# One sequence of attention steps over all pairs of three chunks, beside the first layer's matmuls

## The chip, the cores and the metric

The kernel runs on one core of one Trainium2 chip. The metric is the device time of one execution in microseconds (us). The engines are PE (TensorE, matmuls; PEld is its weight load), DVE (VectorE), ACT (ScalarE), POOL (GpSimd) and SP (SyncE, which here issues every DMA). Each engine has its own sequence of instructions, set at the build.

## What is computed

Attention over tokens that share a hash bucket, and behind it two feed-forward layers. Inputs come as float32, the weights of the layers as float64:

```python
q_bits = (einsum('bhsd,dk->bhsk', q, proj) > 0)     # 2 batches, 8 heads, 768 tokens, 64 wide, 6 bits
mask = q_bucket[:, :, :, None] == k_bucket[:, :, None, :]
scores = where(mask, scale * q @ k.T, -1e9)
attn = exp(scores - max) / (sum + 1e-9)
x = (attn @ v) as 1536 tokens x 512
h = maximum(x @ w_in1, 0);            x = (h * h) @ w_out1      # 512 -> 2048 -> 512
h = x @ w_in2; g = max(h,0) + alpha * min(h,0);   out = g @ w_out2
```

## The kernel before

The 1536 tokens are four chunks of 384 (half a batch each), numbered 0 to 3. The attention of a chunk goes pair of heads by pair of heads, four pairs. A pair (class Pair, line 203) has these steps:

- prepare (line 357): load the pair after this one, hash the keys (only in chunks 0 and 2, where a batch begins) and the queries with small matmuls, split them into a high and a low part, and put them with the mask's codes into the tiles k and q, by DMAs on SP. Two steps in chunks 1 and 3, five in chunk 2.
- scores (line 378), six times, for 2 heads x 3 blocks of 128 queries: four matmuls into a score tile s, DVE's negated maximum `low` (line 389), ACT's exponential into sm with the row sum (line 392).
- p_t (line 399), twice for each block: three PE transposes of sm into an m tile, and a copy to pt by ACT or DVE (lines 411, 413).
- recip (line 431): DVE's reciprocals of the sums, a PE transpose (line 437), a DMA out and one back that spreads them over the partitions (lines 441, 444).
- av (line 415), in three parts of four matmuls, pt times V, into one m tile o; the last part copies it to u.
- finish (line 447): u times the reciprocals on DVE, the high part xh on ACT, the low part xl on POOL.

The first layer of a chunk (feed_forward, line 661) runs over 16 slices f of the 2048 hidden columns: hidden makes 12 matmuls of 384 columns (lines 613 to 615) from xh, xl and the split weights wh, wl; the activation follows on ACT, DVE or POOL; project makes 9 matmuls of 512 columns (lines 641 to 645) into acc. The weights of slice f + 1 are split meanwhile (ACT wh, line 565; DVE or POOL wl, line 566), and float64 weights are converted on ACT and DVE (lines 539 to 544). The second layer is alike.

Chunk 0's attention runs alone, to about 93 us. Then the first layer of chunk c runs with the attention of chunk c + 1 beside it, for c = 0, 1, 2. The layer has 80 slots per chunk, and between its matmuls it calls Background (line 502), which emits so many of the attention's steps that they are spread evenly between its marks. The time in the marks is counted in chunks: chunk 1's steps from 0 to 0.8 (LEAD, line 26), chunk 2's from 0.8 to 1.8, chunk 3's from 1.8 to 2.8. attention(c, 1) (line 461) writes one chunk's steps: a begin and all the preparation of its first pair, then for each block its scores, one step of the next pair's preparation, and the transposes of the block before. Behind the transposes of a pair's last block come recip and all three parts of av, and finish behind the fourth block of the next pair. At the chunk's end all that is left is done before the next chunk's begin.

The order in which these calls are written is a priority: a scheduler sets the order on each engine at the build, and moves an instruction that isn't ready behind others that are. While the first layer runs the score tile is one buffer of PSUM (ps_s) and the m tiles are two (ps_m).

Of the kernel before, what the change touches and what calls it, by code (L numbers as in the profile page):

```python
# [22 lines left out]

EVICT = ("aavaav", "avavav", "vvavva", "vvavva")

LEAD = 0.8


@with_exitstack
def kernel(  # L30
# [26 lines left out]
    NTB = T // P  # L57
    NKB = S // P
    NPAIR = H // 2
    NCH = NT // T  # L60
# [56 lines left out]
    def f32(ap):  # L117
        return ap.bitcast(F32)
# [52 lines left out]
    raw = {}  # L171
# [4 lines left out]
    def load_pair(c, j):  # L176

        b, s0 = c // 2, (c % 2) * T
        h0 = 2 * j
        kr = None  # L180
        if c % 2 == 0:
            kr = p2.tile([P, 2, S], F32, tag="kr", name="kr")
            nc.sync.dma_start(out=kr[:, 1], in_=kT[b, h0:h0 + 2].rearrange("h d s -> (h d) s"))
            if c == 0 and j == 0:
                nc.sync.dma_start(
                    out=proj_sb, in_=proj[:, 0:P].rearrange("p (h n) -> p h n", h=2)[:, :, 0:GR // 2]
                )
        qn = p2.tile([P, T], F32, tag="qn", name="qn")
        nc.sync.dma_start(out=qn, in_=qT[b, h0:h0 + 2, :, s0:s0 + T].rearrange("h d s -> (h d) s"))
        if c % 2 == 0:  # L190
            keys[b, j] = [kr, None, None]
            if c == 0 and j == 0:
                load_values(b, j)
                nc.sync.dma_start(out=ident, in_=eye)
                nc.sync.dma_start(out=alpha_sb, in_=alpha)
        raw[c, j] = qn

    def load_values(b, j):
        vr = p4.tile([P, NKB, 2 * D], F32, tag="vr", name="vr")
        keys[b, j][-1] = vr  # L200
        return nc.sync.dma_start(out=vr, in_=v[b, j])

    class Pair:
# [243 lines left out]
        def finish(self):  # L447
            xh, xl = xT.get(self.c) or new_x(self.c)
            x = self.u
            nc.vector.tensor_tensor(x, x, self.rb, ALU.mult)  # L450
            nc.scalar.activation(xh[:, self.j, :], x, AF.Copy)
            nc.gpsimd.tensor_tensor(xl[:, self.j, :], x, f32(xh[:, self.j, :]), ALU.subtract)  # L452

    def new_x(key):
        xT[key] = (
            m2.tile([P, KDM, T], F32R, tag="xh", name="xh"),
            m2.tile([P, KDM, T], F32R, tag="xl", name="xl"),
        )
        return xT[key]

    def attention(c, lag):

        def begin():
            if (c, 0) not in raw:
                load_pair(c, 0)

        pairs = [Pair(c, j) for j in range(NPAIR)]
        steps = [begin] + pairs[0].prepare()
        late = []
        ended = []  # L470

        def tail():
            pr, h, t = late.pop(0)
            for a in range(2):
                steps.append(lambda a=a: pr.p_t(h, t, a))
            if t == NTB - 1 and h == 1:
                steps.append(pr.recip)
                for part in range(3):
                    steps.append(lambda part=part: pr.av(part))
                ended.append(pr)  # L480

        for j, pr in enumerate(pairs):
            nxt = pairs[j + 1].prepare() if j + 1 < NPAIR else []
            for u in range(2 * NTB):
                h, t = divmod(u, NTB)
                steps.append(lambda pr=pr, h=h, t=t: pr.scores(h, t))
                late.append((pr, h, t))
                for _ in range(2 if c == 0 else 1):
                    if nxt:
                        steps.append(nxt.pop(0))  # L490
                if ended and u == 3:
                    steps.append(ended.pop().finish)
                if len(late) > lag:
                    tail()
        while late:
            tail()
        while ended:
            steps.append(ended.pop(0).finish)
        return steps


    class Background:

# [51 lines left out]
    def keep(u):  # L555

        kept[u] = state["res"].tile([P, DM], F32, name="w%d_%d_%d" % u)
        nc.sync.dma_start(out=kept[u], in_=w_d[u])
# [145 lines left out]
    def second_x(c):  # L704

        cell = []

        def begin():
            new_x((1, c))
            y = state["res"].tile([P, NTB, DM], F32, tag="yb", name="yb")  # L710
            nc.sync.dma_start(out=y, in_=y_d[c])
            cell.append(y)

        def block(t):
            ps = ps_s.tile([P, 2, 512], F32, tag="s", name="s")[:, t % 2, :]
            for m in range(KDM):
                nc.tensor.transpose(ps[:, m * P:(m + 1) * P], cell[0][:, t, m * P:(m + 1) * P], ident)  # L717
            src = ps.rearrange("p (m n) -> p m n", m=KDM)
            xh, xl = xT[1, c]
            hi = xh[:, :, t * P:(t + 1) * P]  # L720
            nc.scalar.activation(hi, src, AF.Copy)
            nc.vector.tensor_tensor(xl[:, :, t * P:(t + 1) * P], src, f32(hi), ALU.subtract)

        return [begin] + [lambda t=t: block(t) for t in range(NTB)]
# [15 lines left out]
    state["moe"] = True  # L740


    steps, marks = [], [(0.0, 0)]
    for c in range(1, NCH):
        steps += attention(c, 1)
        marks.append((c - 1 + LEAD, len(steps)))
    following = Background(steps, marks)
    steps = []
    for f in range(KFF):
        for o in range(2):  # L750
# [19 lines left out]
    steps = [lambda f=f, o=o: keep((1, f, o)) for f in range(KFF) for o in range(2)]  # L770
    conversion = Background(steps, [(0.25, 0), (1.3, len(steps))])
    for n in range(NCH + 1):
        steps = second_x(n) if n < NCH else []
# [76 lines left out]
```

## Time and profile before

| | us |
|---|---|
| median of 3 runs | 845.5 |
| lowest and highest run | 843.67, 845.7 |
| the profiled execution, its own time | 845.31 |
| its span, first to last instruction | 843.5 |
| PE busy in the span | 800.3 (95%) |
| DVE, ACT, POOL busy | 507.3, 473.7, 363.9 |
| first layer of chunk 0 with attention of chunk 1 | 95 to 223 |
| of chunk 1 with attention of chunk 2 | 223 to 369 |
| of chunk 2 with attention of chunk 3 | 369 to 493 |
| first layer of chunk 3, alone | 493 to 564 |

The stretches end where acc is copied out (line 695). Times are counted from the span's start. A busy PE isn't a PE at its peak, since records of matmuls overlap: a row in the lists of instructions in order of time can begin before the one above it has ended.

### The profile page before, as it was taken

The page shows a single profiled execution, that of the slowest core. Times are in us where ns is not written, and L with a number is a line of the kernel's source. Part 1 is how long each engine was busy: PE and PEld are TensorE (multiplying, and loading weights), DVE is VectorE, ACT ScalarE, POOL GpSimd, SP SyncE. Part 2 cuts the span into 40 slices and gives each one's busy share as a digit, 9 for nine tenths or more (in the row PEclk, how much of TensorE's full clock was granted, in tenths as well). Part 3 has the DMA queues.
Part 4 walks back from the last instruction along what each step waited for, and adds up shares of the span by engine and source line. Part 5 has one row for each costly group of instructions (what it writes and reads, how often), then busy time and mean ns, then how long its engine had stood idle before and what let it go on. Part 6 is the DMA issues. An engine that isn't in the chain of part 4 may idle for free.

```text
span 843.5 us, 12642 instructions
## 1 busy us (share of the span) xinstructions
PE 800.3 (95%) x4384; PEld 649.7 (77%) x4384; DVE 507.3 (60%) x822; ACT 473.7 (56%) x926; POOL 363.9 (43%) x321
## 2 busy tenths in 40 slices
PE   6999899999999999999999999999999999999997
PEld 4665777776768767586787789989989998998996
DVE  7678799887447658688897531224435445444442
ACT  5677677776557557475565556654434444444342
POOL 1002233233446646533333345555555555555553
PEclk9999899999999999999999999999999999999999
DMA  6757678775867687587765589600101011001001
GB/s 181 200 154 244 200 245 254 249 241 179 243 194 212 201 231 254 177 280 248 210 203 184 166 295 329 204 38 1 38 1 37 1 39 38 1 1 37 1 1 38
DMA packets 54863, 127.61 MB, mean 151 GB/s; under 512 B 7216, under 2 KB 11600, under 8 KB 54800
## 3 DMA queue, kind: packets, MB, share of 16 engines
q1 hardware_dynamic: 54800, 126.81, 48.1%
q8 instruction: 34, 0.56, 0.3%
q14 instruction: 29, 0.24, 0.1%
HBM read 82.93 MB, written 23.12 MB: 126 GB/s over the span
## 4 chain that ended last, share of the span: by engine, by line
PE 46%; DVE 3%; issue 2%; POOL 1%; ACT 1%; DMA 0%; POOLq 0%; DVEq 0%; ACTq 0%
PE acc L645 7%; PE acc L641 7%; PE acc L642 7%; PE m L615 4%; PE m L613 4%; PE m L614 4%; PE h L613 3%; PE h L615 3%; PE h L614 3%; PE m L423 2%; PE s L384 1%; POOL gl L631 1%; DVE low L389 1%; PE m L407 1%; PE s L717 1%
## 5 line engine op out<-in xcount | busy, mean ns | idle before, releaser
L631 POOL TENSOR_TENSOR gl<-g,gh 128x384 fp32r<-128x384 f32 x128 | 135.8, 1061 | 256.1 <-ACT gh L630 122.7
L641 PE MATMUL acc<-wh,gh 128*128 128x512 f32 x384 | 158.1, 412 | 0.0
L642 PE MATMUL acc<-wl,gh 128*128 128x512 f32 x384 | 151.7, 395 | 0.0
L566 POOL TENSOR_TENSOR wl<-wf,wh 128x512 fp32r<-128x512 f32 x80 | 108.6, 1362 | 99.4 <-ACT wh L565 80.2
L565 ACT ACTIVATE wh<-w 128x512 fp32r<-128x512 f32 x128 | 80.5, 629 | 80.7 <-PE m L614 45.7
L645 PE MATMUL acc<-wh,gl 128*128 128x512 f32 x384 | 116.1, 398 | 2.3 <-POOL gl L631 2.3
L565 ACT ACTIVATE wh<-wf 128x512 fp32r<-128x512 f32 x128 | 79.7, 628 | 58.5 <-PE h L614 23.6
L613 PE MATMUL h<-xh,wh 128*128 128x384 f32 x296 | 106.0, 358 | 1.5 <-ACT r L621 0.8
L389 DVE TENSOR_REDUCE low<-s 128x1 f32<-128x768 f32 x84 | 80.0, 952 | 41.8 <-PE s L384 41.6
L615 PE MATMUL h<-xh,wl 128*128 128x384 f32 x296 | 101.9, 344 | 1.2 <-POOL wl L566 1.2
L614 PE MATMUL h<-xl,wh 128*128 128x384 f32 x296 | 101.2, 342 | 0.6 <-POOL xl L452 0.6
L392 ACT ACTIVATE sm<-s,low 128x768 f32<-128x768 f32 x84 | 75.7, 901 | 33.8 <-DVE low L389 33.4
L384 PE MATMUL s<-k,q 128*128 128x384 f32 x336 | 80.7, 361 | 13.7 <-ACT sm L392 13.6
L645 PEld LDWEIGHTS acc<-wh,gl 128*128 128x128 f32 x384 | 71.7, 188 | 22.5 <-POOL gl L631 5.5
L566 POOL TENSOR_TENSOR wl<-w,wh 128x512 fp32r<-128x512 f32 x64 | 83.1, 1298 | 6.0 <-ACT wh L565 6.0
L641 PEld LDWEIGHTS acc<-wh,gh 128*128 128x128 f32 x384 | 72.3, 188 | 15.8 <-issue 4.8
L407 PE MATMUL m<-ident,sm 128*128 128x128 f32 x531 | 81.8, 275 | 2.2 <-ACT sm L392 1.0
L384 PEld LDWEIGHTS s<-k,q 128*128 128x128 f32 x336 | 58.1, 193 | 31.8 <-ACT sm L392 25.2
L630 ACT ACTIVATE gh<-g 128x384 fp32r<-128x384 f32 x64 | 33.5, 524 | 81.8 <-DVE g L629 81.8
L642 PEld LDWEIGHTS acc<-wl,gh 128*128 128x128 f32 x384 | 72.4, 189 | 8.8
L628 DVE TENSOR_SCALAR r<-m,alpha_sb 128x384 f32<-128x384 f32 x43 | 26.6, 618 | 86.9 <-PE m L615 86.7
L407 PEld LDWEIGHTS m<-ident,sm 128*128 128x128 f32 x531 | 64.9, 141 | 14.0 <-ACT sm L392 2.4
(117 smaller groups left out, 1432.8 us busy)
## 6 DMA issues: line engine op xcount, KB each, us to landing
wf<-w SPq DMA_DIRECT2D x96, 256.0 KB, 3.7
wbits<-in_w_in_dram SPq DMA_DIRECT2D x32, 512.0 KB, 4.0
wbits<-in_w_out_dram SPq DMA_DIRECT2D x32, 512.0 KB, 3.9
q<-q SPq DMA_DIRECT2D x48, 192.0 KB, 3.8
w<-wf SPq DMA_DIRECT2D x32, 256.0 KB, 2.3
w<-we SPq DMA_DIRECT2D x32, 256.0 KB, 2.3
w<-w SPq DMA_DIRECT2D x32, 256.0 KB, 4.5
k<-kh SPq DMA_DIRECT2D x14, 384.0 KB, 5.2
```

The costliest lines, as they stand in the source:

```text
L384: nc.tensor.matmul(ps[:, a, 0:HALF], self.q[:, h, i, qs], self.k[:, h, i, ks], start=i == 0, stop=i == 1)
L389: low_ins = nc.vector.tensor_reduce(low, ps[:, 0:2, 0:HALF], AX.XY, ALU.max, negate=True)
L407: nc.tensor.transpose(ps[:, i * P:(i + 1) * P], pp[:, b * P:(b + 1) * P], ident)
L565: nc.scalar.activation(hi, w, AF.Copy)
L566: engine.tensor_tensor(lo, w, f32(hi), ALU.subtract)
L613: nc.tensor.matmul(hp, wih[:, ks], xh[:, kk, :], start=first, stop=False)
L614: nc.tensor.matmul(hp, wih[:, ks], xl[:, kk, :], start=False, stop=False)
L615: nc.tensor.matmul(hp, wil[:, ks], xh[:, kk, :], start=False, stop=last)
L631: nc.gpsimd.tensor_tensor(gl, g, f32(gh), ALU.subtract)
L641: nc.tensor.matmul(acc[:, t, :], gh[:, blocks[t]], woh, start=first, stop=False)
L642: nc.tensor.matmul(acc[:, t, :], gh[:, blocks[t]], wol, start=False, stop=False)
L645: nc.tensor.matmul(acc[:, t, :], gl[:, blocks[t]], woh, start=False, stop=last)
```

## The change

One function, attention_beside, writes the steps of all twelve pairs of chunks 1 to 3 in one sequence. What was done at a chunk's start and end is now done as between any two pairs: the next chunk's first pair is prepared during the last pair of this one, and the last pair's transposes, recip, av and finish stand among the next chunk's first blocks. Behind a pair's first scores come a step of preparation, the old pair's last transposes, recip and the first part of av; behind its second scores the other two parts of av and the first transposes; no step of preparation there. finish comes behind the sixth block of the next pair (behind the fourth where a chunk ends). LEAD is 0.88, and the marks are the ends of the chunks in that sequence. The rest of the program is as it was.

```diff
-LEAD = 0.8
+LEAD = 0.88
...
+    def attention_beside():
+        pairs = [Pair(c, j) for c in range(1, NCH) for j in range(NPAIR)]
+        steps, ends = [], []
...
+        def turn(pr, u):
+            for a in range(2):
+                steps.append(lambda a=a: pr.p_t(*divmod(u, NTB), a))
...
+        def finish(pr):
+            steps.append(pr.finish)
+            if pr.j == NPAIR - 1:
+                ends.append(len(steps))
+
+        steps += [begin] + pairs[0].prepare()
+        last = 2 * NTB - 1
+        for n, pr in enumerate(pairs):
+            old = pairs[n - 1] if n else None
+            prep = pairs[n + 1].prepare() if n + 1 < len(pairs) else []
+            for u in range(2 * NTB):
+                steps.append(lambda pr=pr, u=u: pr.scores(*divmod(u, NTB)))
+                if prep and u != 1:
+                    steps.append(prep.pop(0))
+                if u == 0 and old:
+                    turn(old, last)
+                    steps.append(old.recip)
+                    values(old, 0)
+                if u == 1 and old:
+                    values(old, 1)
+                    values(old, 2)
+                if u:
+                    turn(pr, u - 1)
+                if u == 4 and prep:
+                    steps.append(prep.pop(0))
+                if u == (3 if old and old.j == NPAIR - 1 else last) and old:
+                    finish(old)
...
-    steps, marks = [], [(0.0, 0)]
-    for c in range(1, NCH):
-        steps += attention(c, 1)
-        marks.append((c - 1 + LEAD, len(steps)))
-    following = Background(steps, marks)
+    steps, ends = attention_beside()
+    following = Background(steps, [(0.0, 0)] + [(c + LEAD, n) for c, n in enumerate(ends)])
```

How this moves the instructions shows at three places. Lines above 550 are some 50 higher in the changed kernel: 665 to 667 are its hidden, 693 to 697 its project, 593 to 596 its conversions, 618 its split.

The first place is DVE from the finishing of chunk 1's last pair (u<-u,rb) on. Before, conversions (wsg, we) and the preparation of chunk 2's first two pairs (bits, kr) follow it:

```order
281 L450 TENSOR_TENSOR u<-u,rb 128x384
282 L566 TENSOR_TENSOR wl_2542<-wf,wh_2541 128x512
283 L239 TENSOR_SCALAR bits<-m 128x192
284 L268 TENSOR_TENSOR kr<-kr,kh 128x768
285 L544 SCALAR_TENSOR_TENSOR we<-we,wsg 128x512
286 L275 TENSOR_SCALAR kr<-s,pop 128x768
287 L239 TENSOR_SCALAR bits<-m 128x96
288 L541 TENSOR_SCALAR wsg<-wbits 128x512
289 L542 SCALAR_TENSOR_TENSOR wsg<-wbits,wsg 128x512
290 L239 TENSOR_SCALAR bits<-m 128x192
291 L268 TENSOR_TENSOR kr<-kr,kh 128x768
292 L695 COPY y<-acc 128x512
```

On the same engine now, from the same instruction on:

```order
287 L450 TENSOR_TENSOR u<-u,rb 128x384
288 L413 COPY pt<-m 128x384
289 L389 TENSOR_REDUCE low<-s 128x1
290 L413 COPY pt<-m 128x384
291 L389 TENSOR_REDUCE low<-s 128x1
292 L593 TENSOR_SCALAR wsg<-wbits 128x512
293 L594 SCALAR_TENSOR_TENSOR wsg<-wbits,wsg 128x512
294 L413 COPY pt<-m 128x384
295 L596 SCALAR_TENSOR_TENSOR we<-we,wsg 128x512
296 L275 TENSOR_SCALAR kr<-s,pop 128x768
297 L593 TENSOR_SCALAR wsg<-wbits 128x512
298 L594 SCALAR_TENSOR_TENSOR wsg<-wbits,wsg 128x512
```

The maxima and copies of chunk 2's first pair, which stood behind the copy of acc (y), have moved ahead of it.

The second place is PE between the second and third block of chunk 2's second pair, before:

```order
687 L384 MATMUL s<-k,q 128x384 x4
688 L407 MATMUL m<-ident,sm 128x128 x6
689 L613 MATMUL h<-xh,wh_2939 128x384
690 L614 MATMUL h<-xl,wh_2939 128x384
691 L615 MATMUL h<-xh,wl_2940 128x384
692 L613 MATMUL h<-xh,wh_2939 128x384
693 L614 MATMUL h<-xl,wh_2939 128x384
694 L615 MATMUL h<-xh,wl_2940 128x384
695 L613 MATMUL h<-xh,wh_2939 128x384
696 L614 MATMUL h<-xl,wh_2939 128x384
697 L615 MATMUL h<-xh,wl_2940 128x384
698 L384 MATMUL s<-k,q 128x384 x4
```

Now, between the third and fourth block of the same pair; ahead of these rows stand the third block's scores and one line-693 and one line-694 matmul:

```order
674 L407 MATMUL m<-ident,sm 128x128 x3
675 L693 MATMUL acc<-wh_2850,gh 128x512
676 L694 MATMUL acc<-wl_2851,gh 128x512
677 L697 MATMUL acc<-wh_2850,gl 128x512 x3
678 L407 MATMUL m<-ident,sm 128x128 x3
679 L665 MATMUL h<-xh,wh_2899 128x384
680 L666 MATMUL h<-xl,wh_2899 128x384
681 L667 MATMUL h<-xh,wl_2900 128x384
682 L665 MATMUL h<-xh,wh_2899 128x384
683 L666 MATMUL h<-xl,wh_2899 128x384
684 L667 MATMUL h<-xh,wl_2900 128x384
685 L384 MATMUL s<-k,q 128x384 x4
```

The work between two blocks' scores has gone from six transposes and nine matmuls of 384 columns to six transposes, seven matmuls of 512 and six of 384.

The third place is PE where chunk 3's second pair ends and its third begins, from the reciprocals' transpose (rin) to the next scores, before:

```order
1202 L437 MATMUL m<-ident,rin 6x128
1203 L641 MATMUL acc<-wh_4726,gh 128x512
1204 L642 MATMUL acc<-wl_4727,gh 128x512
1205 L423 MATMUL m<-pt,vr 64x384 x4
1206 L641 MATMUL acc<-wh_4726,gh 128x512
1207 L642 MATMUL acc<-wl_4727,gh 128x512
1208 L423 MATMUL m<-pt,vr 64x384 x8
1209 L641 MATMUL acc<-wh_4726,gh 128x512
1210 L642 MATMUL acc<-wl_4727,gh 128x512
1211 L645 MATMUL acc<-wh_4726,gl 128x512 x3
1212 L384 MATMUL s<-k,q 128x384 x4
```

On the same engine now, from the first part of av on:

```order
1222 L423 MATMUL m<-pt,vr 64x384 x4
1223 L693 MATMUL acc<-wh_4740,gh 128x512
1224 L694 MATMUL acc<-wl_4741,gh 128x512
1225 L384 MATMUL s<-k,q 128x384 x4
1226 L693 MATMUL acc<-wh_4740,gh 128x512
1227 L694 MATMUL acc<-wl_4741,gh 128x512
1228 L423 MATMUL m<-pt,vr 64x384 x4
1229 L693 MATMUL acc<-wh_4740,gh 128x512
1230 L694 MATMUL acc<-wl_4741,gh 128x512
1231 L697 MATMUL acc<-wh_4740,gl 128x512 x3
1232 L423 MATMUL m<-pt,vr 64x384 x4
```

The twelve matmuls have gone from two runs to three, and the second block's scores have moved in between the first and the second.

## Rows read from the trace of the kernel before

**Rows 1.** Stretches: length, busy us (count) of PE, PEld, DVE, ACT, POOL; clock, DMA.

```profile
95.00:223.00 128.00, 122.55 (x711) 94.17 (x710) 107.11 (x170) 92.52 (x189) 43.62 (x35) 1.00 0.75 235
223.00:369.00 146.00, 138.39 (x796) 103.77 (x794) 97.23 (x142) 87.16 (x175) 80.08 (x67) 0.99 0.73 219
369.00:493.00 124.00, 118.27 (x667) 92.59 (x667) 92.77 (x150) 71.40 (x145) 43.00 (x35) 1.00 0.66 214
...
120.00:140.00 20.00, 19.57 (x118) 15.02 (x112) 19.21 (x30) 16.41 (x35) 6.24 (x5) 1.00 0.82 263
...
200.00:220.00 20.00, 19.34 (x119) 13.41 (x119) 11.19 (x16) 9.48 (x19) 10.15 (x9) 1.00 0.71 200
340.00:360.00 20.00, 18.71 (x106) 12.22 (x107) 12.12 (x18) 9.19 (x18) 10.12 (x10) 0.91 0.62 200
460.00:480.00 20.00, 20.00 (x113) 14.85 (x113) 13.05 (x23) 10.92 (x22) 6.16 (x5) 1.00 0.40 122
```

**Rows 2.** PE's waits, 95 to 493 us: total us, times, longest.

```profile
PE s L384 <- ACT sm L392: 11.0, 18, 1.4
PE m L437 <- DVE pt L413: 2.0, 2, 1.8
...
PE m L437 <- DVE rin L435: 1.1, 2, 0.7
```

**Rows 3.** 163 to 167.5 us in order of time: start, duration, engine, instruction, idle.

```profile
163.24 1.29 POOL L566 TENSOR_TENSOR wl<-wf,wh 128x512 fp32r<-128x512 f32 x1 [2.01 <-ACT wh L565]
...
163.30 1.77 DVE L544 SCALAR_TENSOR_TENSOR wf<-we,wsg 128x512 uint32<-128x512 uint32 x1
...
165.00 0.94 DVE L389 TENSOR_REDUCE low<-s 128x1 f32<-128x768 f32 x1
...
165.98 0.90 ACT L392 ACTIVATE sm<-s,low 128x768 f32<-128x768 f32 x1 [0.21 <-DVE low L389]
...
167.02 0.80 PE L384 MATMUL s<-k,q 128*128 128x384 f32 x3 [1.36 <-ACT sm L392]
```

**Rows 4.** PE in order of time, four places.

```profile
234.25 0.34 PE L614 MATMUL h<-xl,wh 128*128 128x384 f32 x1
234.43 0.86 PE L384 MATMUL s<-k,q 128*128 128x384 f32 x4
...
302.01 0.85 PE L645 MATMUL acc<-wh,gl 128*128 128x512 f32 x3
302.70 0.82 PE L407 MATMUL m<-ident,sm 128*128 128x128 f32 x6
...
119.16 4.09 PE L423 MATMUL m<-pt,vr 128*64 128x384 f32 x24
123.18 0.98 PE L384 MATMUL s<-k,q 128*128 128x384 f32 x4
...
474.06 0.73 PE L645 MATMUL acc<-wh,gl 128*128 128x512 f32 x2
...
474.73 1.51 PE L423 MATMUL m<-pt,vr 128*64 128x384 f32 x8
...
476.17 0.44 PE L613 MATMUL h<-xh,wh 128*128 128x384 f32 x1
```

**Rows 5.** PE in order of time, at 341 us.

```profile
340.98 0.27 PE L437 MATMUL m<-ident,rin 128*6 128x128 f32 x1 [1.80 <-DVE pt L413]
```

**Rows 6.** PE and POOL in order of time, handover of chunk 3's last pair.

```profile
471.72 0.27 PE L437 MATMUL m<-ident,rin 128*6 128x128 f32 x1
...
481.53 1.20 POOL L452 TENSOR_TENSOR xl<-u,xh 128x384 fp32r<-128x384 f32 x1 [4.66 <-ACT xh L451]
```

**Rows 7.** PE, SP and POOL in order of time, handover of another pair.

```profile
307.93 0.27 PE L437 MATMUL m<-ident,rin 128*6 128x128 f32 x1
...
314.53 0.33 SPq L441 DMA_DIRECT2D rin<-rrow  x1
...
328.76 1.48 POOL L452 TENSOR_TENSOR xl<-u,xh 128x384 fp32r<-128x384 f32 x1
```

More of the change, by code (lines that the diff above doesn't have):

```diff
@@ L499, in attention, with begin, values @@
         return steps
+    def attention_beside():
+        pairs = [Pair(c, j) for c in range(1, NCH) for j in range(NPAIR)]
+        steps, ends = [], []
+        def begin():
+            if (1, 0) not in raw:
+                load_pair(1, 0)
+        def turn(pr, u):
+            for a in range(2):
+                steps.append(lambda a=a: pr.p_t(*divmod(u, NTB), a))
+        def values(pr, part):
+            steps.append(lambda: pr.av(part))
+        def finish(pr):
[24 more added lines that the diff above has]
+                    finish(old)
+            assert not prep
+        turn(pr, last)
+        steps.append(pr.recip)
+        for part in range(3):
+            values(pr, part)
+        finish(pr)
+        return steps, ends
     class Background:
```

## The prediction

> **What bounds the kernel now.** The stretches come first. The change touches only the three stretches in which the first layer of chunks 0, 1 and 2 runs and the attention of chunks 1, 2 and 3 runs beside it: 95 to 223, 223 to 369 and 369 to 493 us. TensorE (PE) is busy there for 122.55 of 128, 138.39 of 146 and 118.27 of 124; the fullest other engine is DVE with 107.11, 97.23 and 92.77 [rows 1]. So PE sets the time of these stretches. Its matmuls are the same before and after, and what can change is the time in which it doesn't start one: 18.8 us of idle time by the records, plus what the records hide (below).
>
> Next the waits. Of PE's waits in these 398 us the largest by far is that of a score matmul for ACT's exponential: 11.0 us in 18 waits, then the transposes of the reciprocals for DVE, 3.1 us in 4 [rows 2]. The cause of the first is the score tile. While the first layer runs there is one (ps_s, one buffer, lines 72 and 101), and the next block's four matmuls can't start until DVE's maximum and ACT's exponential of the block before have read it. [Rows 3] show one case in order of time: POOL's split starts at 163.24, DVE's conversion at 163.30 takes 1.77 us beside it, the maximum behind it on DVE starts at 165.00, the exponential runs from 165.98 to 166.88, and PE starts the scores at 167.02 after 1.36 us idle. The idle column is too small: a matmul of 384 columns has a record of 0.34 us, but four that follow each other take 0.86 us, so they start (0.86 - 0.34) / 3 = 0.173 us apart, and the record before each wait covers 0.17 us in which another could have started [rows 4]. The 18 waits therefore cost 11.0 + 18 x 0.17 = 14.1 us.
>
> **The score waits.** After its scores a block needs 0.94 us on DVE, 0.90 us on ACT, about 0.04 us from the one to the other and 0.14 us from the exponential's end to the next scores, all read from the starts and ends in [rows 3]. That is at least 2.0 us; the case shown there, with 1.7 us in DVE's queue ahead of the maximum, needs 3.7 us. PE must have that much other work standing between two blocks. I added it up from the order: 0.173 us for a matmul of 384 columns, 0.23 for one of 512, 0.11 for a transpose, 4.0 us for a pair's twelve attention-value matmuls, all from [rows 4]. Of the 72 blocks, the work ahead of the next scores was under 2.5 us for 25 and is now for 9; it was under 3 us for 48 and is now for 27. The change's four to six steps do stand between two scores, but not everywhere. By chunk the count under 3 us goes from 19, 16 and 13 to 16, 5 and 6. Chunk 1 hardly changes, chunks 2 and 3 do, because they get the empty stretches, in which no attention ran: from 200 to 220 us DVE does 11.19 us of work, against 19.21 in a full slice [rows 1].
>
> If the waits fall with the count under 2.5 us, 14.1 x 16/25 = 9.0 us go; if with the count under 3 us, 14.1 x 21/48 = 6.2 us. I take the middle, **-7.6 us**. The bounds are wider: -11 if chunks 2 and 3 lose all of theirs, -4 if the queues ahead of the maximum grow a little.
>
> **The attention-value matmuls in more pieces.** The change puts the first third of a pair's twelve after the next pair's first scores, and the other two thirds after its second scores. On PE's order they stand in 28 unbroken runs for these 12 pairs before, and in 35 now. A run of twelve (24 records, since each makes two) takes 4.02 us from its start to the next matmul, 119.16 to 123.18. The last pair has three runs of four, and one takes 1.44 us, 474.73 to 476.17; three make 4.32, so a break costs 0.15 us on that side. On the entry side two matmuls of 512 columns ahead of a run take 0.67 us instead of 0.46 [rows 4]. A break is then 0.15 to 0.36 us; I take 0.3, and 7 of them are **+2.1 us** (1.0 to 2.5).
>
> **The clock.** From 340 to 360 us the granted clock is 0.91, that is 3.6 us at the lower of the two levels, 1.2 instead of 2.4 GHz, or (1 - 0.91) x 20 = 1.8 us of work lost [rows 1]. Just ahead of it stands PE's longest wait of the three stretches, 1.80 us at 341 us, for DVE's copy [rows 5]; it isn't one of the score waits that I expect to go, but they fill the same queue, so I take half, **-0.9 us** (0 to -1.8).
>
> **What I cost at nothing.** The reciprocals' transposes: the PE work between the last transposes of probabilities and them is 0.6 us in the mean before and 0.7 now, so their waits stay as they are, within 2 us either way. The finishing of a pair (DVE, ACT, POOL, one instruction each) moves from the fourth to the sixth block of the next pair, and is covered by at least a block of other work. The output tile of a pair keeps one of the two m banks from the first to the last of its attention-value matmuls, 6.8 us of PE work instead of 5.5; no transposes stand in between in either order, so nobody wants the bank. The two calls of begin that go issue no instruction, as the pair is loaded already. SP's queue holds the same DMAs in a slightly different order; those of K and Q now come about six blocks ahead of their use at a chunk's start too, instead of right ahead of it. If that cover were gone, the cost would be the slow case of the second rival.
>
> **The sum.** -7.6 + 2.1 - 0.9 = -6.4 us. The profiled execution took 845.31 us, of which 843.5 is the span; the median of the runs is 845.5. That gives 838.9, rounded to **839.0 us**.
>
> **Rival 1, slower: DVE in the first stretch.** The new work there is chunk 2's first pair (six maxima, its copies, the key preparation). If it lands where DVE is full already, every wait ahead of a maximum grows. Place: 95 to 223 us. Price: 16 gaps of chunk 1 stay under 3 us, so each further 0.1 us of turnaround costs 1.6 us. With the turnaround 0.85 us longer, half of what the queue of [rows 3] added, it is 13.6 us, and the time 852.6. From 0.4 us the gain is gone. For it: DVE at 19.21 of 20 us [rows 1]. Against it: the work goes in from about 200 us on, where DVE is half empty. 0.14.
>
> **Rival 2, no change: the handover of the last chunk.** Chunk 3's last attention-value matmul now stands 8.7 us of PE work ahead of the first matmul that needs the chunk, against 13.9 before, and the reciprocals' transpose 16 us ahead of it. In the trace this handover took from 471.72 to 482.73, 11.0 us [rows 6], and fits. Another pair's took from 307.93 to 330.24, 22.3 us, since SP issued the reciprocals' DMA only at 314.53 [rows 7]. Were the last pair that slow, PE would wait 22.3 - 16 = 6.3 us, and the time would be 845.3. For it: nothing in the program keeps SP's queue short there. Against it: the DMA engines' share is 0.40 from 460 to 480 us, and 0.62 from 340 to 360 [rows 1], and the other two handovers have 21 us of cover. 0.12.
>
> **Rival 3, slower: the clock falls where attention-value matmuls are broken up.** If each of the 7 new breaks drew a fall like the one of [rows 1], that would be 7 x 1.8 = 12.6 us, and the time 851.6. Against it: the last pair's three runs, from 472 to 479 us, went with a granted clock of 1.00 [rows 1, 4]. 0.02. The Trainium skill, in Perfetto Trace Analysis, section Matmul Optimizations, says that it is important for matmuls to execute back to back in batches, because the engine scales its power with use. That rule speaks against splitting a batch; the row at 460 us doesn't bear it out, where PE was busy for the whole slice.
>
> **Rival 4, no change: the spacing doesn't reach the chip.** The waits of chunks 2 and 3 could come from the queues of DVE and ACT alone, whatever PE has in hand, as in the case of [rows 3], where about 3.1 us of PE work stood ready and didn't do. Then the scores' term is near -2, the breaks cost 2.1, and the time is 845.3. 0.08.
>
> **How the numbers follow.** The forecast has 0.64. The sum's own bounds are -11 + 1.0 - 1.8 - 2 = -13.8 and -4 + 2.5 + 2 = +0.5, that is 831.5 to 845.8. With rivals 2 and 4 inside and the lower part of rival 1 at the edge, the range is 831 to 847. A measurement of this kernel can tell about 0.3%, 2.5 us, from no change. Faster than that is the forecast, 0.64; within it are rivals 2 and 4, 0.20; slower are rivals 1 and 3, 0.16.
>
> **What would show it.** PE's wait of the scores for the exponential should be about 5 us in under 10 waits, most of them before 223 us. Chunks 2 and 3 should lose theirs. No score-free stretch of 20 us should be left, and DVE's busy time by slices should be flatter. The attention-value groups should show more and shorter runs with the clock at 1.00. No wait for xh or xl over 1 us should stand at the start of a chunk's first layer. I am wrong if the waits in chunk 1 grow, if PE waits longer for DVE's copies or for POOL's splits than now, or if a handover stalls.

## The result and the profile after

| | before | after |
|---|---|---|
| median, us (4 runs each) | 845.6 | 836.63 |
| lowest and highest run | 843.67, 848.57 | 836.36, 839.12 |
| the profiled execution, its span | 845.31, 843.5 | 836.36, 834.6 |
| first layer of chunks 0, 1, 2 ends at | 222.7, 369.4, 493.3 | 233.1, 367.7, 483.5 |

The ratio is 0.9907 with the interval 0.9881 to 0.9934, which is 7.9 us (5.6 to 10.1); the medians lie 9.0 us apart and the profiled executions 8.9. At the end of the third stretch the lead is 9.8 us; chunk 3's first layer and the second layer give back 0.9.

The stretches of after, in the columns of [rows 1]; their borders have moved, because a chunk's attention now begins earlier:

```profile
95.00:233.00 138.00, 132.79 (x800) 101.95 (x799) 118.32 (x189) 100.67 (x210) 45.52 (x36) 1.00 0.79 238
233.00:368.00 135.00, 129.06 (x748) 98.05 (x748) 89.50 (x138) 81.19 (x166) 76.92 (x66) 1.00 0.74 230
368.00:484.00 116.00, 114.48 (x630) 88.02 (x629) 81.50 (x134) 67.69 (x136) 41.30 (x35) 1.00 0.65 203
```

PE is idle for 5.2 + 5.9 + 1.5 = 12.7 us by the records, against 18.8 in [rows 1]. The slices that answer to those of [rows 1]:

```profile
120.00:140.00 20.00, 19.33 (x120) 15.03 (x121) 19.74 (x30) 15.07 (x31) 6.57 (x5) 1.00 0.82 258
200.00:220.00 20.00, 19.73 (x112) 14.35 (x111) 13.93 (x20) 12.91 (x26) 8.37 (x8) 1.00 0.64 183
340.00:360.00 20.00, 18.94 (x114) 15.85 (x112) 15.87 (x23) 12.99 (x28) 10.23 (x10) 1.00 0.79 264
```

The slice at 200 us has more DVE work, 13.93 us, and the clock at 340 us is at the higher level throughout. PE's waits from 95 to 484 us, as in [rows 2]:

```profile
PE s L384 <- ACT sm L392: 5.7, 11, 1.0
PE s L251 <- ACT sm L392: 1.5, 1, 1.5
PE m L407 <- ACT q L317: 1.3, 2, 1.1
PE s L384 <- DVE kr L275: 1.2, 2, 0.9
PE m L407 <- DVE bits L239: 1.2, 2, 0.6
PE m L437 <- DVE rin L435: 0.6, 1, 0.6
```

The score waits for the exponential fell from 11.0 us in 18 to 5.7 in 11. By chunk they went from 2.6, 2.5 and 5.9 us to 2.9, 1.0 and 1.8: chunks 2 and 3 lost most of theirs, chunk 1 did not. New are waits of transposes for an m tile that the hashing (bits) or the query's codes (q) still hold, and of scores for the score tile while DVE reads the next pair's key codes from it (kr).

The longest stretches without a score matmul were 28.2 us (from 194.2) and 21.0 us (from 334.2) before; now none is over 9.8 us. That was one of the prediction's signs. Another was that most of the score waits would stand before 223 us; about half do.

Idle records leave out starts that come late under a running record. So I also took all intervals between PE's starts in the three stretches, less the prediction's price for each instruction (0.173 us, 0.23, 0.11 and so on), and put what was left to the instruction that came late. Its rows are estimates, since they hang on these prices:

| PE's late starts, us | before | after |
|---|---|---|
| scores | 19.5 | 13.0 |
| reciprocals' transposes | 4.8 | 1.0 |
| hidden and project | 7.7 | 4.7 |
| probabilities' transposes | 2.7 | 4.9 |
| attention-value matmuls, with the clock's fall in before (1.65) | 0.5 | 0.9 |
| hashing and keys | 6.4 | 6.8 |
| sum | 41.6 | 31.3 |

The difference, 10.3 us, is the stage's 9.8 within the rounding and the records that are missing.

### The profile page after: what moved, and what is told of

The parts are those of the page before. It is cut to its first block, busy times and chain, and to the rows that moved or that the text cites. A ratio compares the mean times of both kernels' runs of the same rounds, so it can differ in the third digit from the quotient of the medians.

```text
span 834.6 us, 12635 instructions
## 1 busy us (share of the span) xinstructions
PE 796.7 (95%) x4384; PEld 646.4 (77%) x4384; DVE 499.6 (60%) x822; ACT 472.4 (57%) x926; POOL 360.8 (43%) x321
## 4 chain that ended last, share of the span: by engine, by line
PE 53%; DVE 4%; DMA 3%; ACT 3%; issue 2%; POOL 1%; POOLq 0%; DVEq 0%; SPq 0%; ACTq 0%
PE acc L697 8%; PE acc L693 8%; PE acc L694 7%; PE m L667 4%; PE m L665 4%; PE m L666 4%; PE h L665 4%; PE h L666 3%; PE h L667 3%; PE m L423 3%; DMA w<-we 2%; PE s L384 2%; PE m L407 2%; DVE we L596 1%; DVE low L389 1%
## 5 line engine op out<-in xcount | busy, mean ns | idle before, releaser
L693 PE MATMUL acc<-wh,gh 128*128 128x512 f32 x384 | 159.9, 416 | 0.0
L697 PE MATMUL acc<-wh,gl 128*128 128x512 f32 x384 | 113.8, 396 | 1.8 <-POOL gl L683 1.8
L407 PE MATMUL m<-ident,sm 128*128 128x128 f32 x531 | 85.3, 276 | 3.8 <-ACT q L317 1.3
```

What stands on the lines that cost most here:

```text
L407: nc.tensor.transpose(ps[:, i * P:(i + 1) * P], pp[:, b * P:(b + 1) * P], ident)
L693: nc.tensor.matmul(acc[:, t, :], gh[:, blocks[t]], woh, start=first, stop=False)
L697: nc.tensor.matmul(acc[:, t, :], gl[:, blocks[t]], woh, start=False, stop=last)
```

## The experiments

The times are medians; each ratio is to the kernel before in runs on the same chip (medians 844.97 for the first four, 845.16 for the next four, 845.47 for the last four), with its 95% interval. "Waits" are PE's in the three stretches.

**LEAD alone**, in the kernel before:

```diff
-LEAD = 0.8
+LEAD = 0.88
```

> The kernel before with LEAD at 0.88 and nothing else. On PE's order the blocks with under 3 us of work ahead of the next scores go from 19, 16 and 13 (chunks 1, 2, 3) to 18, 12 and 15, and a stretch of 24 us without scores is left. Theory (one sequence over the chunks fills the empty stretches): 843 to 847 us, score waits of PE near 11 us. Rival (the later mark brings the gain): 838 to 840 us.

841.32 us, 0.9958 [0.9942, 0.9973]. The prediction had no term for this number, and it brings 3.6 us by itself. Its largest wait:

```profile
PE s L384 <- ACT sm L392: 9.7, 12, 1.6
```

Score waits are 1.3 us below [rows 2], and the clock doesn't fall at 341 us as in [rows 1]; the long wait of [rows 5] isn't there either. The stretches without a score are as long as before, 30.0 us from 200.3 and 23.1 us from 337.8.

**The sequence with the old LEAD**, 0.8 in the changed kernel:

> The changed kernel with LEAD back at 0.8. Blocks under 3 us: 13, 6 and 3. Theory (the sequence brings the gain): 835 to 839 us, score waits at or under the changed kernel's 6.9 us. Rival (the later mark): 842 to 845 us.

837.51 us, 0.9903 [0.988, 0.9926], with score waits of 7.8 us in 9. Within a microsecond of the change itself: inside the sequence LEAD is worth next to nothing, though alone it was worth 3.6.

**The sequence with the old order inside a pair**: everything of the change but the places of av, preparation and finish.

```diff
-                if prep and u != 1:
+                if prep:
                     steps.append(prep.pop(0))
+                if u == 3 and old:
+                    finish(old)
                 if u == 0 and old:
                     turn(old, last)
                     steps.append(old.recip)
-                    values(old, 0)
-                if u == 1 and old:
-                    values(old, 1)
-                    values(old, 2)
+                    for part in range(3):
+                        values(old, part)
                 if u:
                     turn(pr, u - 1)
-                if u == 4 and prep:
-                    steps.append(prep.pop(0))
-                if u == (3 if old and old.j == NPAIR - 1 else last) and old:
-                    finish(old)
```

> One sequence over the twelve pairs with the order inside a pair as before: a step of preparation behind each of the first five blocks, all three parts of av behind the first block, finish behind the fourth. Blocks under 3 us: 19, 9 and 8; av in 31 runs. Theory (the sequence): 837 to 840 us, most of the gain. Rival (the new order inside a pair brings it): 843 to 846 us.

836.11 us, 0.9892 [0.9871, 0.9913]: as fast as the change, whose two measurements are 836.63 and 837.18.

```profile
PE s L384 <- ACT sm L392: 7.1, 11, 2.1
```

Blocks with under 3 us of PE work behind them number 36, against 27 with the change and 48 before, yet its waits are only 1.4 us longer than the change's, and it saves breaks (31 unbroken runs of av on PE, not 35). Its longest stretch without a score is 15.5 us. The four to six steps between two blocks' scores bring nothing that could be measured.

**The new order chunk by chunk**: the same loop as the change's over one chunk's four pairs at a time, LEAD 0.88; here against the kernel before.

```diff
-LEAD = 0.8
+LEAD = 0.88
...
+    def attention_beside(c):
+        pairs = [Pair(c, j) for j in range(NPAIR)]
...
     for c in range(1, NCH):
-        steps += attention(c, 1)
+        steps += attention_beside(c)[0]
```

> The new order inside a pair, but chunk by chunk: each chunk's first pair is prepared at its start, and its last pair's transposes, recip, av and finish come at its end. LEAD is 0.88. Blocks under 3 us: 15, 15 and 13; av in 35 runs; a stretch of 25 us without scores. Theory (the sequence): 844 to 849 us, no gain, and the cost of seven more breaks in av. Rival (the order inside a pair): 837 to 840 us.

840.25 us, 0.9943 [0.9924, 0.9962]: 1.1 us under LEAD alone, whose interval it overlaps. It has stretches of 31.9 and 19.5 us without a score. With the run above: at LEAD 0.88 the one sequence brings 841.3 - 836.1 = 5.2 us, the order inside a pair about nothing.

**av in one piece**, behind the second block's scores of the changed kernel:

```diff
-                    values(old, 0)
                 if u == 1 and old:
-                    values(old, 1)
-                    values(old, 2)
+                    steps.append(lambda old=old: [old.av(part) for part in range(3)])
```

> The changed kernel with a pair's three parts of av in one step behind the second block's scores. On PE's order av stands in 18 runs instead of 35; blocks under 3 us of work ahead of the next scores are 17, 6 and 6 (16, 5 and 6 in the changed kernel). Theory (a break in av costs 0.3 us, as the prediction had it): 17 x 0.3 = 5.1 us less, about 831 us. Rival (PE's time at a break is made up elsewhere, or twelve av matmuls on end hold up others): 835 to 838 us.

840.81 us, 0.9947 [0.9929, 0.9965]: 4 us slower than the change. The breaks are saved (18 runs of av for 35; by the starts that is 4.1 us), but more is lost in waits:

```profile
PE s L384 <- ACT sm L392: 12.5, 13, 2.8
PE s L251 <- ACT sm L392: 2.8, 1, 2.8
```

With the waits for kr, 13.7 us stand ahead of scores, against 6.9 with the change. They don't stand at the gap that av had filled: 11.1 us are ahead of a pair's fifth and sixth blocks, and none ahead of its second or third. Why they grew there is not shown. At 253.8 us the clock falls for 3.4 us, behind the wait of line 251.

**The same in the old order**, av in one step behind the first block's scores of the sequence, here against the version with the old order inside a pair:

```diff
-                    for part in range(3):
-                        values(old, part)
+                    steps.append(lambda old=old: [old.av(part) for part in range(3)])
```

> One sequence with the old order inside a pair, and av in one step behind the first block: 14 runs of av instead of 31, blocks under 3 us 18, 9 and 8. Theory (0.3 us for a break): 17 x 0.3 = 5.1 us under the same kernel with av in three steps, about 831 us. Rival: 835 to 838 us.

830.64 us, 0.9834 [0.9808, 0.986]: 5.5 us under the same sequence with three steps, and the fastest of all. Its stretches, its score waits, and a run of av:

```profile
95.00:230.00 135.00, 130.69 (x794) 102.87 (x793) 117.59 (x187) 100.66 (x211) 44.84 (x37) 1.00 0.78 240
230.00:365.00 135.00, 126.09 (x754) 99.62 (x753) 97.04 (x138) 80.06 (x161) 79.23 (x67) 1.00 0.75 233
365.00:477.00 112.00, 109.78 (x624) 87.59 (x623) 85.96 (x135) 66.98 (x137) 41.98 (x34) 1.00 0.65 207
```

```profile
PE s L384 <- ACT sm L392: 9.1, 12, 1.6
```

```profile
119.30 4.09 PE L423 MATMUL m<-pt,vr 128*64 128x384 f32 x24
123.32 0.97 PE L384 MATMUL s<-k,q 128*128 128x384 f32 x4
```

PE idles for 15.4 us in these stretches, 13.6 with three steps, and is busy for 366.6, against 374.4 there. Runs of av go from 31 to 14, and 5.5 / 17 = 0.32 us for a break lies within what [rows 4] gave (0.15 to 0.36).

The traces price a break directly. At the higher clock and without a wait, a run of 4 av matmuls takes 1.44 us to the next matmul's start in every version that has one, a run of 8 takes 2.73 and one of 12 takes 4.02, so each break costs (3 x 1.44 - 4.02) / 2 = 0.15 us inside. The first matmul of a run comes 0.10 us late, by the median in each of the traces; the 0.21 us of [rows 4] was one place. Together that is 0.25 us for a break, or 4.2 of the 5.5 us; the rest is other waits or scatter.

**finish behind the fourth block** of every pair, as before, in the changed kernel:

```diff
-                if u == (3 if old and old.j == NPAIR - 1 else last) and old:
+                if u == 3 and old:
```

> The changed kernel with every finish behind the fourth block, as before, not the sixth. It tells what such a small move is worth, and how far the time scatters when the order changes a little. Theory (finish is covered): within 1 us of the changed kernel, 835.5 to 837.5 us. Rival (the later finish spares DVE a wait for the reciprocals' DMA): 838 us or more.

839.84 us, 0.9934 [0.9909, 0.996], but its eight runs go from 835.7 to 842.6, and the profiled one, 837.34, has score waits of 5.6 us in 9 and no wait that the change lacks. Inconclusive: the median speaks for 3 us and so for the rival, but no line of the trace says what they are.

**More work for DVE in the first stretch** (rival 1): the second layer's conversions start earlier in the changed kernel.

```diff
-    conversion = Background(steps, [(1.0, 0), (NCH - 1.1, len(steps))])
+    conversion = Background(steps, [(0.6, 0), (NCH - 1.5, len(steps))])
```

> The changed kernel with the conversion of the second layer's weights spread from 0.6 to 2.5 chunks instead of 1.0 to 2.9. That puts 0.4 / 1.9 of 32 conversions, some 7 with 2.3 us of DVE work each, or 15 us, into the first stretch, where DVE is busy for 118 of 138 us. Theory of the prediction's first rival (DVE's queue ahead of the maximum sets the score waits of the first stretch): the first stretch grows, its score waits double, and the time is 840 us or more. Rival (PE's own order sets them): 835 to 838 us.

847.26 us, 1.0019 [1.0003, 1.0034]: 10.6 us slower than the change, but not where I had aimed. Only three more conversions landed in the first stretch, and it grew by 1.1 us; the second grew by 13.3:

```profile
95.00:234.00 139.00, 133.12 (x794) 101.69 (x793) 121.18 (x196) 101.82 (x211) 44.91 (x35) 1.00 0.77 239
234.00:382.00 148.00, 133.76 (x757) 100.21 (x755) 101.04 (x145) 84.39 (x170) 78.64 (x67) 0.99 0.75 230
```

```profile
PE s L384 <- ACT sm L392: 7.8, 14, 1.5
PE h L667 <- POOL wl L618: 4.4, 8, 1.2
...
PE acc L697 <- POOL gl L683: 1.7, 2, 1.4
```

So DVE at 121.18 of 139 us costs PE little. In the second stretch PE waits for POOL's splits, of which the change's list of waits has none, and chunk 2's waits for the score tile went from 2.2 to 5.3 us. By share neither POOL (78.64 of 148 us, 76.92 of 135 with the change) nor DVE (101.04, 89.50) is much fuller there. What differs is the order: three stretches without a score of 16.0 to 18.6 us are back, and the clock falls for 3.4 us at 303.7 us. Rival 1's place wasn't tested as meant, and this run doesn't show its mechanism either.

**av in one piece in the kernel before**:

```diff
-                for part in range(3):
-                    steps.append(lambda part=part: pr.av(part))
+                steps.append(lambda: [pr.av(part) for part in range(3)])
```

> The kernel before with a pair's three parts of av in one step and nothing else; av in 16 runs instead of 28, blocks under 3 us of work 18, 11 and 13 instead of 19, 16 and 13. Theory (a break in av costs 0.3 us by itself, whatever the sequence): 12 x 0.3 = 3.6 us less, and some for the blocks, 839 to 842 us. Rival (whole av pays only in one sequence over the chunks): 844 to 846 us.

845.19 us, 1.0007 [0.9984, 1.0029]: nothing. The 12 saved breaks (16 runs for 28, 3.0 us at 0.25) went into waits, of 13.1 us for the exponential where [rows 2] had 11.0, and of av itself for the copies behind which it is now called at once:

```profile
PE s L384 <- ACT sm L392: 13.1, 16, 2.3
PE m L423 <- DVE pt L413: 2.5, 3, 1.2
```

**The changed kernel again**, beside the last two:

> The changed kernel once more, beside the others on one chip, for the scatter: 836 to 839 us.

837.18 us, 0.9897 [0.9876, 0.9918]; score waits 5.4 us in 10. The result stands.

**LEAD in the fastest version**, 0.95 and 0.8 for 0.88:

> One sequence, old order inside a pair, av in one step, LEAD 0.95. Blocks under 3 us: 16, 6 and 5 instead of 18, 9 and 8 with 0.88. Theory (score waits follow that count): 828 to 831 us. Rival (the handover of the last chunk, with its last av 4.0 us of PE work ahead of the chunk's first matmul instead of 8.7): 832 us or more, with a wait for xh or xl at the start of a chunk's first layer.

> The same with LEAD 0.8. Blocks under 3 us: 17, 8 and 5. Theory (the sequence matters, the mark hardly): 829 to 832 us. Rival (the later mark matters as it did without the sequence, 3.6 us): 834 us or more.

With 0.95 it takes 838.07 us, 0.9907 [0.9888, 0.9927], with 0.8 833.32 us, 0.9861 [0.9834, 0.9888]. 0.88 keeps the lowest median, but the intervals of 0.88 and 0.8 overlap; the profiled execution at 0.8 has one more fall of the clock, 3.4 us from 349.6 on, inside a score wait of 3.1 us. At 0.95 no wait at the last handover appeared. Its score waits and two of four slices with a lower clock:

```profile
PE s L384 <- ACT sm L392: 10.1, 11, 2.1
```

```profile
160.00:180.00 20.00, 19.04 (x107) 15.15 (x109) 18.17 (x31) 15.96 (x34) 7.17 (x5) 0.91 0.74 220
300.00:320.00 20.00, 18.19 (x104) 13.45 (x103) 11.45 (x18) 9.65 (x21) 9.44 (x8) 0.91 0.66 211
```

The clock takes 1.8 us in each, 3.6 of the 6.2 us by which the span is longer than at 0.88. The rest is scattered over scores, projections and hashing, and I can't name its cause.

## Why the prediction was right, and where it wasn't

**The bound** held. PE is the fullest engine in every stretch of every version, and what changed is the time in which it starts nothing.

**The score waits** were the right mechanism at the right places: chunks 2 and 3, not chunk 1. Of the -7.6 us, -6.5 came by the starts, and -5.0 by the prediction's own count (11.1 us in 19 to 6.9 in 14, with the waits for kr and with those too short for the lists above, 0.17 us more for each). What remains is the case of [rows 3] again, with PE's work between the two blocks used up; after, from 323 us in order of time:

```profile
323.57 1.74 POOL L618 TENSOR_TENSOR wl<-wf,wh 128x512 fp32r<-128x512 f32 x1
...
324.08 0.94 DVE L389 TENSOR_REDUCE low<-s 128x1 f32<-128x768 f32 x1
...
325.06 0.90 ACT L392 ACTIVATE sm<-s,low 128x768 f32<-128x768 f32 x1 [2.23 <-DVE low L389]
...
326.10 0.96 PE L384 MATMUL s<-k,q 128*128 128x384 f32 x4 [0.96 <-ACT sm L392]
```

Here the maximum started when a conversion ended on DVE (from 322.82 on, 1.33 us), and from its start to the scores it took 2.0 us, as worked out.

The **count of blocks** under 3 us, with which I sized the term, isn't a law. Over the versions: 48 blocks and 11.1 us of idle score records before, 45 and 9.8 (LEAD alone), 43 and 8.1 (chunk by chunk), 36 and 7.2 (old order), 35 and 10.6 (old order, av whole), 29 and 13.7 (changed, av whole), 27 and 6.9 (the change), 22 and 8.3 (LEAD 0.8). That the term came near was partly luck: the count ignores when DVE gets to the maximum, and which gaps av fills.

**The breaks**: 7 at the 0.25 us that the traces show are 1.7 us, for 2.1 predicted; in the table of starts the row grew by 0.4 + 1.65 = 2.05 us, since the clock's fall lay in these matmuls before and has gone. The prediction's upper bound for a break rested on one place of [rows 4] that isn't typical. After, a pair's run in two pieces, with the second block's scores in between:

```profile
143.61 1.51 PE L423 MATMUL m<-pt,vr 128*64 128x384 f32 x8
145.05 0.44 PE L384 MATMUL s<-k,q 128*128 128x384 f32 x1
...
146.57 0.87 PE L423 MATMUL m<-pt,vr 128*64 128x384 f32 x4
```

**The clock**: -1.65, nearly the whole of what stood in [rows 1] at 340 us, for -0.9. I had reasoned that the wait of [rows 5] wasn't among those to go; it went too.

**Costed at nothing** was wrong, with both signs. The reciprocals' transposes came to -3.8 us by the starts (by the records 3.4 us in 5 waits to 0.6 in 1). I had left them at nothing within 2 us, because the PE work ahead of them is the same 0.6 to 0.7 us; but 2.0 of the 3.1 us in [rows 2] were waits for DVE's copies of pt, which points to DVE's queue at that place rather than to PE's work. With LEAD 0.8 in the sequence 1.4 us of them are back, in two waits: part of the gain hangs on how the instructions happen to fall. Hidden and project gained 3.0 us, 1.7 of it by the records in waits for POOL's splits, which I hadn't priced; before:

```profile
PE h L615 <- POOL wl L566: 1.2, 2, 0.7
...
PE acc L645 <- POOL gl L631: 0.5, 2, 0.3
```

The transposes of probabilities lost 2.2 us; 2.5 us of waits after are for m tiles that the next pair's hashing and query codes hold.

**LEAD** had no term, and alone brings 3.6 us. It doesn't do so by the prediction's mechanism, as the empty stretches stay. By the records it takes 1.3 us from the score waits, 1.6 from those of the reciprocals' transposes, and the clock's 1.7; so in the sum it hides inside the score term, the clock and what was costed at nothing. Inside the sequence it brings next to nothing, so the gains of the two overlap. The forecast of 838.9 was 2.5 us above the profiled execution: scores +1.1, clock -0.75, reciprocals -3.8, hidden and project -3.0, transposes +2.2, hashing +0.4 and 0.9 given back later are -2.95, the rest rounding. What I had left out is -6.8 us on the one side and +3.5 on the other, so the sum was better than its parts.

**Rival 1** (DVE in the first stretch) didn't occur: at 120 us DVE is busy for 19.74 of 20, as in [rows 1], and chunk 1's waits are 2.9 us for 2.6. **Rival 2** (the last handover) didn't: from the reciprocals' transpose to the end of the split it took 466.51 to 478.26, 11.8 us, within its 16:

```profile
466.51 0.27 PE L437 MATMUL m<-ident,rin 128*6 128x128 f32 x1
...
477.24 1.02 POOL L452 TENSOR_TENSOR xl<-u,xh 128x384 fp32r<-128x384 f32 x1 [1.05 <-ACT xh L451]
```

**Rival 3** fell: the clock is 1.00 in all three stretches, the broken runs among them. The rule of the Trainium skill (Perfetto Trace Analysis, section Matmul Optimizations) that matmuls belong in back-to-back batches isn't borne out here by way of the clock; whole batches of av paid in one order, cost in another, and brought nothing in the kernel before. **Rival 4** fell for chunks 2 and 3; but since the order inside a pair brings nothing that could be measured, nothing here speaks against it for the part of the change that sets the four to six steps.

What stays open: why av whole adds waits at a pair's fifth and sixth blocks in the new order and less in the old, how LEAD alone gains, why LEAD 0.95 is slower, and the scatter of finish behind the fourth block.

## What to carry to other kernels

Where one stage of background work ends and the next begins, look for a stretch in which the filler is missing, and write the filler as one sequence over all stages: here this was worth 5 us beyond LEAD, and the finer order inside it nothing that could be measured. Price the waits at the boundary of every engine's queue, not of the largest alone: the small ones that I left at nothing moved 6.8 us one way and 2.6 the other. Keeping the twelve attention-value matmuls in one run saves 0.25 us for each break, but measure it in the order at hand: it was worth 5.5 us in one order, nothing in another, and cost 4 us in a third.

## What the runs showed of the hardware

A vector instruction on tiles in SBUF mostly takes longer where a POOL instruction is already running when it starts. In the kernel before, from 93 to 115 us, DVE's conversion of line 542 takes 683 ns at least, 688 in the median and 1668 at most, and that of line 544 takes 682 to 695; the one of [rows 3] took 1.77 us, started 0.06 us behind POOL's split and ended 0.54 us after it. In the early-conversion kernel the first of its two forms, line 594, by stretch (length, DVE's busy us and count, clock):

```profile
95.00:234.00 139.00, 21.37 (x29) 1.00 0.77 239
234.00:382.00 148.00, 16.40 (x18) 0.99 0.75 230
```

That is 737 ns each where POOL is busy for 32% of the time, and 911 where it is busy for 53%. The Trainium skill (SBUF — State Buffer, section SBUF: two separate sides) says that DVE and GpSimd take a shared pair of ports as an exclusive lock, a DVE instruction with two inputs in SBUF among those concerned. The trace agrees with that, and shows it for an instruction with one tensor input too, line 541's. In the kernel before, from 95 to 497 us, line 541 takes 0.42 us by the median where POOL is idle (30 times) and 1.11 where a POOL instruction is running at its start (23 times); line 542 takes 0.69 (35) and 1.28 (12). DVE's reads of PSUM tiles don't change: its maximum takes 0.95 us and its copy of an m tile 0.55 either way. One long case of line 541, and one with POOL idle:

```profile
304.43 2.52 POOL L566 TENSOR_TENSOR wl<-wf,wh 128x512 fp32r<-128x512 f32 x2 [1.91 <-ACT wh L565]
...
305.76 1.48 DVE L541 TENSOR_SCALAR wsg<-wbits 128x512 uint32<-128x512 uint32 x1
```

```profile
165.87 0.41 DVE L541 TENSOR_SCALAR wsg<-wbits 128x512 uint32<-128x512 uint32 x1
```

No run here took POOL's work away to show it alone.

The clock fell at long waits of PE or soon behind them: in [rows 5] after 1.80 us, and in the version with LEAD 0.95 at 162.2 and 308.9 us behind these:

```profile
160.96 0.96 PE L384 MATMUL s<-k,q 128*128 128x384 f32 x4 [2.07 <-ACT sm L392]
```

```profile
307.71 0.44 PE L662 MATMUL h<-xh,wl 128*128 128x384 f32 x1 [1.81 <-POOL wl L613]
```

The sequence in the old order had a wait of 2.1 us and no fall in the three stretches. With av whole in the changed kernel there were two waits of 2.8 us, ending at 253.9 and 357.7 us, and the clock fell at the first alone (0.91 from 240 to 260 us, 1.00 from 340 to 360). So a wait's length alone doesn't decide it.

Two versions that differ by LEAD alone differ by microseconds that no single wait explains (837.5 and 836.6; 830.6, 833.3 and 838.1). A gain of 2 us from reordering steps can't be put down to its stated reason on this kernel without such neighbours.
